# Luna attention and MoE on one core: v of batch 1 loaded ahead of its q, and another order of steps

## The chip, the cores and the metric

The kernel runs on one core of a Trainium2 chip. The time is that of the device for one execution, in microseconds (us). The engines are TensorE (PE; its weight loads are shown as PEld), VectorE (DVE), ScalarE (ACT), GpSimd (POOL) and SyncE (SP). Each works through its own instructions in their order in the program; semaphores make one wait for another.

## The reference

For 8 batches of 8 heads, with 576 positions of 64 channels and 32 packed positions:

```python
def sm_attn(qq, kk, vv):
    s = scale * np.matmul(qq, kk.transpose(0, 1, 3, 2))
    s = s - np.max(s, axis=-1, keepdims=True)
    a = np.exp(s)
    a = a / (np.sum(a, axis=-1, keepdims=True) + 1e-09)
    return np.matmul(a, vv)
p_packed = sm_attn(p, k, v)
out = sm_attn(q, p_packed, p_packed)
```

The result, with heads side by side as 4608 rows x of 512, goes through an MLP with 2048 hidden channels:

```python
h = x @ w_in
r = np.maximum(h, 0.0)
g = s * (r * r) + b
return (g @ w_out).astype(np.float32)
```

## The kernel before

The kernel works batch by batch. For a batch b it makes the scores of p against k and their exponentials, sums v with them into 32 packed values per head, scores q against the packed values, and normalizes. It does not form the attention's output: since that is weights times packed values, it multiplies the packed values by w_in first (`packed_w`, giving pw) and then pw by the weights (aT), which gives the hidden layer in one step (`mlp_in`). After relu and square (gT), 16 matmuls of 512 columns for each 128 rows give an output tile (`Out.step`, the yps rows of the profile).

The order is written out by hand. Each of PE's, DVE's, ACT's, POOL's and SP's instructions is pinned to the order in which the program issues it, and a string of words gives that order. In the profile nearly every instruction therefore bears a helper's line (L62 for matmuls, L65 for transposes, L73 for the rest). The words, with b the batch:

- `Lk`, `Lq`, `Lv`, `Lp1`, `Lpall`, `Lwi`, `Lwo`: loads on POOL's DMA queue (w_in and w_out in quarters; a quarter of w_out serves four of an output tile's 16 matmuls). Each of kn, qn and vn has one buffer, so that a load waits until the batch before has been read. Each load also waits for the landing of the one eight before it.
- `Tkb.h`, `Tqb.h`: transposes of half of k or q on PE and their copy to kT or qT; batches 0 and 1 only. `Dk`, `Dq`: the same by a transposing DMA on SP for the later batches.
- `PD`, `PP`, `PA`, `PPA`: doubling of p and its transposes, of batch 0 and 1 and of all others.
- `V`: copy of v into vr on DVE. `Fb.a`: first scores and their exponential. `P`: the packed values on PE (pps), their reciprocal and scaling on DVE (pk). `X`: two transposes of pk and the copy to ppd. `S`: second scores and their exponentials on ACT.
- `Ab.a`: sums of the exponentials on PE, then logarithm (ld) and reciprocal (rcd) on ACT and their product aT on DVE; in batch 0 by halves of the columns, with the product in a word of its own, `G0.h`.
- `Wb.c`: packed values times w_in into pw, one chunk of 512 columns in batch 0 and two in the others. Chunk 0 of batch 0 is copied in two halves; `E` is the second.
- `h0.m.h` and `Mb.m`: the hidden layer of two times 128 channels for half of the columns, or of 128 channels for all 576, each four matmuls of 288 columns, then relu on ACT (some on DVE) and square on DVE.
- `Ob.txn`: the next n of the 16 matmuls of output tile t. `BT`, `BC`: sums over w_out's rows for the bias, copied by DVE to biasrep, multiplied on PE and scaled by DVE.
- `Zn`: n matmuls of zeros, 512 columns, whose result nobody reads. `Yn`: the same into the PSUM buffer that the next step will take.

PSUM has two pools: psh with two buffers of two banks (the tiles hps, taken in turn by T, F, S, A, W, h, M, BT and BC, each freed by the engine that reads it), and psy with four (output tiles, packed values, single W chunks and Z).

Up to the string stand the loads of batch 0, the constants and 12 Z. After it the last output tile is done in two halves.

Of the kernel before, what the change touches and what calls it, by code (L numbers as in the profile page):

```python
# [14 lines left out]
def kernel(  # L15
# [14 lines left out]
    B, H, S, D = q.shape  # L30
# [3 lines left out]
    P = 128  # L34
# [10 lines left out]
    HS = S // 2  # L45
# [9 lines left out]
    ysp = ctx.enter_context(tc.tile_pool(name="ysp", bufs=3))  # L55
# [5 lines left out]
    def mm(*a, **kw):  # L61
        return tc.keep_in_program_order(nc.tensor.matmul(*a, **kw))  # L62
# [12 lines left out]
    vec, act, pool, sp = (Pinned(e) for e in (nc.vector, nc.scalar, nc.gpsimd, nc.sync))  # L75
# [280 lines left out]
    def packed_w(b, chs):  # L356
        if b not in pw:
            pw[b] = atp.tile([P, 2, DFF], BF16, tag="pw", name="pw")
        where = {}
        if len(chs) > 1:  # L360
            pair = [big() for _ in range(2)]
            where = {(a, x): pair[a][:, x, :] for a in range(2) for x in range(2)}
        if len(chs) != 2:
            single = [psy.tile([P, NB], F32, tag="y", name="wps") for _ in range(2)]
            where.update({(a, len(chs) - 1): single[a][:] for a in range(2)})
        for x, ch in enumerate(chs):
            for g in range(4):
                for a in range(2):
                    mm(
                        where[a, x][NP * g:NP * g + NP],  # L370
                        ppd[b % 2][D * a:D * a + D, a, g, :],
                        w_in_sb[D * a:D * a + D, g, ch * NB:(ch + 1) * NB],
                        start=True,
                        stop=True,
                        tile_position=(D * a, NP * g),
                    )
        if len(chs) > 1:
            for a in range(2):
                dst = pw[b][:, a, chs[0] * NB:(chs[0] + 2) * NB].rearrange("p (i f) -> p i f", f=NB)
                evict(dst, pair[a][:], a == 0)  # L380
        if len(chs) != 2:
            ch = chs[-1]
            if ch == 0:
                s2["w"] = single
                first_w(b, 0)
                return
            for a in range(2):
                evict(pw[b][:, a, ch * NB:(ch + 1) * NB], single[a][:], a == 0)

    def first_w(b, half):  # L390

        cols = slice(2 * P * half, 2 * P * half + 2 * P)
        for a in range(2):
            vec.tensor_copy(out=pw[b][:, a, cols], in_=s2["w"][a][:, cols])

    def evict(out, in_, on_act):
        if on_act:
            act.copy(out=out, in_=in_)
        else:
            vec.tensor_copy(out=out, in_=in_)  # L400


    def slot(b):
        return 1 if b % 2 else (b % 4)
# [4 lines left out]
    def mlp_in_half(b, m, hf):  # L409

        hps = big()
        cols = slice(hf * HS, (hf + 1) * HS)
        for i in range(2):
            for a in range(2):
                mm(
                    hps[:, i, 0:HS],
                    pw[b][:, a, (m + i) * P:(m + i + 1) * P],
                    aT[b][:, a, cols],
                    start=(a == 0),
                    stop=(a == 1),  # L420
                )
        rlu = ysp.tile([P, 2, HS], BF16, tag="rlu", name="rlu")
        if hf == 0 and m == 0:
            vec.tensor_scalar_max(out=rlu[:], in0=hps[:, :, 0:HS], scalar1=0.0)
        else:
            act.activation(out=rlu[:], in_=hps[:, :, 0:HS], func=AF.Relu)
        g0 = slot(b) * S + hf * HS
        vec.tensor_tensor(out=gT[:, m:m + 2, g0:g0 + HS], in0=rlu[:], in1=rlu[:], op=ALU.mult)

    def mlp_in(b, m):  # L430
        hps = big()
        for a in range(2):
            for hf in range(2):
# [7 lines left out]
        rlu = ysp.tile([P, 2, HS], BF16, tag="rlu", name="rlu")
        if b == 0 and m % 4 == 2:
            vec.tensor_scalar_max(out=rlu[:], in0=hps[:, :, 0:HS], scalar1=0.0)
        else:
            act.activation(out=rlu[:], in_=hps[:, :, 0:HS], func=AF.Relu)
        g0 = slot(b) * S
        vec.tensor_tensor(
            out=gT[:, m, g0:g0 + S].rearrange("p (a s) -> p a s", a=2),
            in0=rlu[:], in1=rlu[:], op=ALU.mult,
        )  # L450
# [118 lines left out]
    def run(word):  # L569
# [71 lines left out]
        out=identb[:], in_=identb[:], compare_op=ALU.not_equal, fill=1.0, base=0,  # L641
# [19 lines left out]
    idle(12, NB)  # L661

    for word in """
        Lwi0 Lwi1 Lwi2 Lwi3 Lwo0 Lwo1 Lp1 Tk0.0 Z10 PD Tk0.1 Lk1 PP0 Z3 F0.0 V0.0 F0.1 Z5 P0.0 V0.1 P0.1
        Z2 Tq0.0 Z1 X0 Z1 Tq0.1 Lq1 Lv1 Lwo2 Lwo3 Lpall Z4 S0 Z3 A0.0 W0.0 Z1 A0.1 G0.0 E Z1 h0.0.0 W0.1
        G0.1 h0.2.0 Y2 h0.0.1 h0.2.1 W0.2 M0.4 W0.3 M0.5 M0.6 O0.0x1 M0.7 O0.0x3 M0.8 M0.9 O0.1x1 PD1
        O0.0x1 M0.10 M0.11 O0.0x3 O0.1x1 PP1 M0.12 O0.1x2 Tk1.0 Tk1.1 Lk2 O0.1x2 M0.13 O0.1x1 F1.0
        O0.1x1 Tq1.0 O0.2x1 Tq1.1 O0.2x1 F1.1 O0.2x2 V1 Lv2 Lq2 M0.14 P1.1 M0.15 O0.2x3 O0.0x2 X1 O0.0x2
        O0.1x1 S1 O0.1x3 O0.2x1 BT PA A1.0 O0.0x3 BC A1.1 O0.1x3 O0.2x3 W1.0 O0.0x1 O0.1x1 O0.2x5 W1.2
        V2 O0.3x6 M1.0 PPA M1.1 M1.2 Dq2 Dk2 Lk3 Lv3 Lq3 O0.3x9 M1.3 M1.4 O0.3x1 O1.0x1 M1.5 M1.6 O1.0x2  # L670
        M1.7 M1.8 O1.0x2 M1.9 M1.10 O1.0x2 M1.11 M1.12 O1.0x2 M1.13 M1.14 O1.0x2 M1.15 O1.0x2 F2.0 F2.1
        O1.0x3 O1.1x3 P2.1 O1.1x5 X2 O1.1x3 S2 O1.1x4 A2.0 O1.1x1 O1.2x1 A2.1 O1.2x7 W2.0 O1.2x8 O1.3x1
        V3 O1.3x1 W2.2 O1.3x6 M2.0 O1.3x1 M2.1 O1.3x1 M2.2 O1.3x1 M2.3 Dq3 Dk3 Lk4 Lv4 Lq4 O1.3x1 M2.4
        O1.3x1 M2.5 O1.3x1 M2.6 O1.3x1 M2.7 O1.3x1 M2.8 O1.4x1 M2.9 O1.4x1 M2.10 O1.4x1 M2.11 O1.4x1
        M2.12 O1.4x1 M2.13 O1.4x1 M2.14 O1.4x1 M2.15 O1.4x9 O2.0x6 F3.0 F3.1 O2.0x6 P3.1 O2.0x4 O2.1x1
        X3 O2.1x5 W3.0 O2.1x6 W3.2 O2.1x4 O2.2x2 S3 O2.2x4 A3.0 O2.2x2 V4 A3.1 O2.2x8 O2.3x8 M3.0 M3.1
        Dq4 Dk4 Lk5 Lv5 Lq5 O2.3x2 M3.2 M3.3 O2.3x2 M3.4 M3.5 O2.3x2 M3.6 M3.7 O2.3x2 M3.8 M3.9 O3.0x2
        M3.10 M3.11 O3.0x2 M3.12 M3.13 O3.0x2 M3.14 M3.15 O3.0x8 F4.0 F4.1 O3.0x2 O3.1x4 P4.1 O3.1x5 X4
        O3.1x3 S4 O3.1x4 A4.0 O3.2x2 A4.1 O3.2x7 W4.0 O3.2x7 O3.3x2 V5 W4.2 O3.3x6 M4.0 O3.3x2 M4.1 M4.2
        O3.3x2 M4.3 Dq5 Dk5 Lk6 Lv6 Lq6 O3.3x4 M4.4 M4.5 O3.4x2 M4.6 M4.7 O3.4x2 M4.8 M4.9 O3.4x2 M4.10  # L680
        M4.11 O3.4x2 M4.12 M4.13 O3.4x2 M4.14 M4.15 O3.4x6 O4.0x6 F5.0 F5.1 O4.0x6 P5.1 O4.0x4 O4.1x1 X5
        O4.1x5 S5 O4.1x4 A5.0 O4.1x2 A5.1 O4.1x4 O4.2x3 W5.0 O4.2x7 V6 O4.2x5 W5.2 O4.2x1 O4.3x5 M5.0
        M5.1 O4.3x2 M5.2 Dq6 Dk6 Lk7 Lv7 Lq7 M5.3 O4.3x2 M5.4 M5.5 O4.3x2 M5.6 M5.7 O4.3x2 M5.8 M5.9
        O4.3x2 M5.10 M5.11 O4.3x1 O5.0x1 M5.12 M5.13 O5.0x2 M5.14 M5.15 O5.0x12 F6.0 F6.1 O5.0x1 O5.1x5
        P6.1 O5.1x5 X6 O5.1x3 S6 O5.1x3 O5.2x1 A6.0 O5.2x2 A6.1 O5.2x7 W6.0 O5.2x6 O5.3x3 V7 W6.2 O5.3x6
        M6.0 O5.3x2 M6.1 M6.2 O5.3x2 M6.3 Dq7 Dk7 M6.4 O5.3x2 M6.5 M6.6 O5.3x1 O5.4x1 M6.7 M6.8 O5.4x2
        M6.9 M6.10 O5.4x2 M6.11 M6.12 O5.4x11 M6.13 M6.14 O6.0x2 M6.15 O6.0x5 F7.0 F7.1 O6.0x6 P7.1
        O6.0x3 O6.1x2 X7 O6.1x4 S7 O6.1x4 A7.0 O6.1x2 A7.1 O6.1x4 O6.2x3 W7.0 O6.2x12 W7.2 O6.2x1 O6.3x5
        M7.0 M7.1 O6.3x2 M7.2 M7.3 O6.3x2 M7.4 M7.5 O6.3x2 M7.6 M7.7 O6.3x2 M7.8 M7.9 O6.3x2 M7.10 M7.11
        O6.3x1 O7.0x1 M7.12 M7.13 O7.0x2 M7.14 M7.15 O7.0x13 O7.1x16 O7.2x16 O7.3x16 O7.4x16  # L690
    """.split():
        run(word)
    while not todo[B - 1, NT].done:
# [29 lines left out]
```

## Time and profile before

| | |
|---|---|
| median of 6 runs | 250.93 us (250.44 to 251.0) |
| the profiled execution | 250.98 us |
| its span in the profile | 249.2 us |
| PE busy | 235.9 us (95%), 2251 matmuls recorded |
| DVE busy | 144.3 us (58%) |
| ACT busy | 138.9 us (56%) |
| POOL busy | 29.1 us (12%) |
| output matmuls (yps) | 138.4 us busy |
| hidden-layer matmuls (hps from aT, pw) | 76.3 us busy |
| zero matmuls (zps) recorded | 40, 12.9 us busy |
| chain that ended last | PE 80%, DMA 16% |

The span runs from the first to the last recorded instruction; about 1.8 us of the time lie around it. Matmuls are pipelined, so the busy time of one, 0.37 us for 512 columns, is longer than the distance from its start to the next start; where PE is the bound, the distance counts. A few matmul records are missing in the trace, which makes some distances look doubled. A row of the timeline gives start and duration in us, engine, line, operation, output and inputs with their shape, how many were merged, and in brackets the idle time of the engine before it with what ended it.

### The profile page before, as it was taken

What the parts mean: (1) busy time and instruction counts of PE and PEld (TensorE: products, weight loads), DVE (VectorE), ACT (ScalarE), POOL (GpSimd) and SP (SyncE); (2) the same over time, 40 slices, a digit from 0 to 9 for tenths busy, and PEclk for the clock granted to TensorE, in tenths of its full rate; (3) what the DMA queues carried; (4) which work ended last, traced back from release to release, by engine and by line L of the source; (5) the groups of instructions that cost most, each with busy time, mean ns of one, the idle gap of its engine ahead of it and who ended that gap; (6) DMA issues with size and microseconds to landing.
All of it is one profiled execution on the core that took longest, in us unless ns stands there. A gap on an engine that the chain in (4) does not pass through costs nothing.

```text
span 249.2 us, 5458 instructions
## 1 busy us (share of the span) xinstructions
PE 235.9 (95%) x2251; PEld 132.5 (53%) x2291; DVE 144.3 (58%) x278; ACT 138.9 (56%) x218; POOL 29.1 (12%) x43
## 2 busy tenths in 40 slices
PE   8796998999999999999999999999999999999994
PEld 2452565446653665356544665466545654366453
DVE  4338768399638673566548672577347642767221
ACT  2156753558856882568655763678375844577000
POOL 8642212000300030000300030000200000000000
PEclk9999999999999999999999999999999999999999
DMA  3999999999498969429898959468996911121133
GB/s 31 199 205 206 204 204 205 196 203 207 90 203 182 208 97 216 110 56 140 153 223 173 214 74 223 91 122 142 164 235 149 143 42 45 42 46 42 42 87 86
DMA packets 59450, 35.50 MB, mean 142 GB/s; under 512 B 32160, under 2 KB 54944, under 8 KB 59424
## 3 DMA queue, kind: packets, MB, share of 16 engines
q0 software_dynamic: 25184, 18.61, 50.1%
q1 hardware_dynamic: 34192, 16.49, 29.4%
q8 instruction: 18, 0.29, 0.5%
q14 instruction: 8, 0.07, 0.1%
q10 hardware_dynamic: 48, 0.03, 0.0%
HBM read 37.23 MB, written 9.44 MB: 187 GB/s over the span
## 4 chain that ended last, share of the span: by engine, by line
PE 80%; DMA 16%; issue 2%; POOL 0%; DVE 0%; POOLq 0%
PE yps L62 48%; PE hps L62 31%; DMA w_out_sb<-in_moe_w_out_dram 8%; DMA w_in_sb<-in_moe_w_in_dram 6%; DMA kn<-in_k_dram 3%; PE pps L62 1%; PE pps L65 1%; POOL kn L73 0%; DVE ysb L73 0%; POOL identb L73 0%; POOLq L73 0%; POOLq L707 0%
## 5 line engine op out<-in xcount | busy, mean ns | idle before, releaser
L62 PE MATMUL yps<-w_out_sb,gT 128*128 128x512 bf16 (+1 forms) x555 | 138.4, 373 | 3.7 <-issue 2.1
L73 ACT ACTIVATE rlu<-hps 128x576 bf16<-128x576 f32 x124 | 75.6, 649 | 28.5 <-PE hps L62 25.8
L62 PEld LDWEIGHTS <-gT 128*128 128x128 bf16 x592 | 54.8, 98 | 50.0 <-issue 8.0
L62 PE MATMUL hps<-aT,pw 128*128 128x288 bf16 x512 | 76.3, 285 | 2.5 <-DVE aT L73 2.3
L73 DVE TENSOR_TENSOR gT<-rlu 128x576 bf16<-128x576 bf16 x128 | 58.0, 458 | 31.0 <-ACT rlu L73 27.4
L62 PEld LDWEIGHTS <-pw 128*128 128x128 bf16 x512 | 49.4, 97 | 29.4 <-issue 4.4
L73 DVE SCALAR_TENSOR_TENSOR ysb<-yps,svec,biasrep 128x512 f32<-128x512 f32 (+1 forms) x37 | 26.9, 733 | 22.4 <-PE yps L62 18.1
L73 ACT ACTIVATE e<-hps 96x768 bf16<-96x768 f32 (+2 forms) x34 | 21.8, 693 | 30.3 <-PE hps L62 30.2
L73 ACT CAST pw<-hps 128x1024 bf16<-128x1024 f32 x14 | 14.2, 1012 | 16.4 <-PE hps L62 15.7
L73 DVE TENSOR_TENSOR aT<-e,rcd 128x576 bf16<-128x576 bf16 x16 | 12.1, 756 | 18.0 <-ACT rcd L73 18.0
L73 POOL DMA_DIRECT2D kn<-in_k_dram x9 | 6.9, 770 | 129.9 <-DMA kT<-kn 101.1
L73 DVE CAST pw<-hps 128x1024 bf16<-128x1024 f32 x14 | 17.1, 1219 | 2.7 <-PE hps L62 2.7
L62 PE MATMUL zps<-zb 128*128 128x512 bf16 x40 | 12.9, 450 | 1.6 <-DVE zb L73 1.2
L73 ACT ACTIVATE ld<-hps 128x576 f32<-128x576 f32 x16 | 10.3, 643 | 2.3 <-PE hps L62 1.6
L73 ACT ACTIVATE rcd<-ld 128x576 f32<-128x576 f32 x16 | 10.9, 683 | 0.5
L62 PEld LDWEIGHTS <-ppd 64*32 64x32 bf16 x384 | 3.5, 89 | 10.3 <-issue 6.9
L62 PE MATMUL hps<-w_in_sb,ppd 64*32 64x512 bf16 x224 | 8.8, 381 | 0.0
L73 DVE RECIPROCAL rd<-pps 128x2 f32<-128x2 f32 x8 | 1.4, 170 | 12.6 <-PE pps L62 12.6
L62 PEld LDWEIGHTS <-kT 128*128 128x128 bf16 x192 | 6.9, 98 | 2.4 <-issue 0.6
L73 DVE COPY vr<-vn 96x3072 bf16<-96x3072 bf16 (+1 forms) x9 | 7.7, 860 | 0.3 <-DMA vn<-in_v_dram 0.3
L62 PEld LDWEIGHTS <-zb 128*128 128x128 bf16 x45 | 4.5, 110 | 6.4 <-issue 3.2
L73 POOL DMA_DIRECT2D vn<-in_v_dram x9 | 6.8, 751 | 7.2 <-DVE vr L73 4.6
(58 smaller groups left out, 100.7 us busy)
## 6 DMA issues: line engine op xcount, KB each, us to landing
out_dram<-ysb SPq DMA_DIRECT2D x23, 192.0 KB, 2.5
kn<-in_k_dram POOLq DMA_DIRECT2D x7, 576.0 KB, 6.4
qn<-in_q_dram POOLq DMA_DIRECT2D x7, 576.0 KB, 12.5
vn<-in_v_dram POOLq DMA_DIRECT2D x7, 576.0 KB, 9.2
out_dram<-ysb SPq DMA_DIRECT2D x24, 128.0 KB, 2.4
w_in_sb<-in_moe_w_in_dram POOLq DMA_DIRECT2D x4, 512.0 KB, 13.6
w_out_sb<-in_moe_w_out_dram POOLq DMA_DIRECT2D x4, 512.0 KB, 18.8
out_dram<-ysb SPq DMA_DIRECT2D x23, 64.0 KB, 2.0
```

The source lines that it names most:

```text
L62: return tc.keep_in_program_order(nc.tensor.matmul(*a, **kw))
L65: return tc.keep_in_program_order(nc.tensor.transpose(*a, **kw))
L73: return lambda *a, **kw: tc.keep_in_program_order(f(*a, **kw))
```

## The change

Three things change in the code. `mlp_in_half` and `mlp_in` share a new function for relu and square; `packed_w` asks for batch 0 before it takes its branch for chunk 0; and the string of words is another one.

In the opening, `Lv1` moves from behind `Lq1` to behind `V0.1`, so that v of batch 1 is issued before its q. The fillers are spread differently: 33 Z in the string instead of 31, and 11 Y instead of 2. `W0.1` stands before `E` and `h0.0.0`, `W0.2` before `h0.0.1`, `W0.3` before `M0.4`. In batch 1 both `Tq` stand behind `P1.1`, and their second half first; `F1.1` follows `F1.0` with one output matmul between; `V1` and `M0.14`, `M0.15` stand before `P1.1`; `A1.0` stands before `BT`, `A1.1` before `BC`. In batch 2, `M1` steps and output matmuls alternate one by one, and `W2.0` is later. The later batches have other places too, with the same steps: in batch 3, S and A before W; in batches 4 and 6, W before or around S; in batch 7, `W7.2` behind `M7.7`, and the first three output tiles interleaved with the last hidden steps.

The code, cut:

```diff
-            if ch == 0:
+            if b == 0 and ch == 0:
                 s2["w"] = single
                 first_w(b, 0)
                 return
...
+    def squared(out, hps, on_vec):
+
+        h = hps[:, :, 0:HS]
         rlu = ysp.tile([P, 2, HS], BF16, tag="rlu", name="rlu")
-        if hf == 0 and m == 0:
-            vec.tensor_scalar_max(out=rlu[:], in0=hps[:, :, 0:HS], scalar1=0.0)
+        if on_vec:
+            vec.tensor_scalar_max(out=rlu[:], in0=h, scalar1=0.0)
         else:
-            act.activation(out=rlu[:], in_=hps[:, :, 0:HS], func=AF.Relu)
-        g0 = slot(b) * S + hf * HS
-        vec.tensor_tensor(out=gT[:, m:m + 2, g0:g0 + HS], in0=rlu[:], in1=rlu[:], op=ALU.mult)
+            act.activation(out=rlu[:], in_=h, func=AF.Relu)
+        vec.tensor_tensor(out=out, in0=rlu[:], in1=rlu[:], op=ALU.mult)
```

The string, up to batch 2 and at the places of the later batches that are spoken of:

```diff
-        Lwi0 Lwi1 Lwi2 Lwi3 Lwo0 Lwo1 Lp1 Tk0.0 Z10 PD Tk0.1 Lk1 PP0 Z3 F0.0 V0.0 F0.1 Z5 P0.0 V0.1 P0.1
-        Z2 Tq0.0 Z1 X0 Z1 Tq0.1 Lq1 Lv1 Lwo2 Lwo3 Lpall Z4 S0 Z3 A0.0 W0.0 Z1 A0.1 G0.0 E Z1 h0.0.0 W0.1
-        G0.1 h0.2.0 Y2 h0.0.1 h0.2.1 W0.2 M0.4 W0.3 M0.5 M0.6 O0.0x1 M0.7 O0.0x3 M0.8 M0.9 O0.1x1 PD1
-        O0.0x1 M0.10 M0.11 O0.0x3 O0.1x1 PP1 M0.12 O0.1x2 Tk1.0 Tk1.1 Lk2 O0.1x2 M0.13 O0.1x1 F1.0
-        O0.1x1 Tq1.0 O0.2x1 Tq1.1 O0.2x1 F1.1 O0.2x2 V1 Lv2 Lq2 M0.14 P1.1 M0.15 O0.2x3 O0.0x2 X1 O0.0x2
-        O0.1x1 S1 O0.1x3 O0.2x1 BT PA A1.0 O0.0x3 BC A1.1 O0.1x3 O0.2x3 W1.0 O0.0x1 O0.1x1 O0.2x5 W1.2
-        V2 O0.3x6 M1.0 PPA M1.1 M1.2 Dq2 Dk2 Lk3 Lv3 Lq3 O0.3x9 M1.3 M1.4 O0.3x1 O1.0x1 M1.5 M1.6 O1.0x2
...
+        Lwi0 Lwi1 Lwi2 Lwi3 Lwo0 Lwo1 Lp1 Tk0.0 Z10 PD Tk0.1 Lk1 PP0 Z3 F0.0 V0.0 F0.1 Z5 P0.0 V0.1 Lv1
+        P0.1 Z1 Tq0.0 Z1 X0 Z2 Tq0.1 Lq1 Lwo2 Lwo3 Lpall Z3 S0 Z3 A0.0 Z2 W0.0 Z2 A0.1 G0.0 Z1 W0.1 E Y1
+        h0.0.0 G0.1 Y4 h0.2.0 W0.2 Y4 h0.0.1 Y1 h0.2.1 W0.3 Y1 M0.4 M0.5 M0.6 O0.0x1 M0.7 O0.0x3 M0.8
+        M0.9 O0.1x1 PD1 O0.0x1 M0.10 M0.11 O0.0x3 O0.1x1 PP1 M0.12 O0.1x2 Tk1.1 Tk1.0 Lk2 O0.1x2 M0.13
+        O0.1x1 F1.0 V1 Lv2 O0.1x1 F1.1 O0.2x2 M0.14 O0.2x1 M0.15 P1.1 O0.2x1 Tq1.1 Tq1.0 Lq2 O0.2x1 X1
+        O0.2x3 O0.0x3 S1 O0.0x1 O0.1x3 A1.0 O0.1x1 BT PA A1.1 O0.0x3 O0.1x3 BC O0.2x4 W1.0 O0.0x1 O0.1x1
+        O0.2x4 W1.2 V2 O0.3x6 M1.0 PPA M1.1 M1.2 Dq2 Dk2 Lk3 Lv3 Lq3 O0.3x9 M1.3 O0.3x1 M1.4 O1.0x1 M1.5
...
+        O5.1x5 X6 O5.1x4 W6.0 O5.1x1 O5.2x5 W6.2 O5.2x6 S6 O5.2x4 A6.0 O5.2x1 O5.3x1 A6.1 V7 O5.3x15
+        M6.0 M6.1 O5.4x1 Dq7 Dk7 O5.4x1 M6.2 M6.3 O5.4x2 M6.4 M6.5 O5.4x2 M6.6 M6.7 O5.4x2 M6.8 M6.9
...
+        O6.0x2 O6.1x3 X7 O6.1x4 S7 O6.1x4 A7.0 O6.1x2 A7.1 O6.1x3 O6.2x16 W7.0 O6.3x7 M7.0 M7.1 O6.3x2
+        M7.2 M7.3 O6.3x2 M7.4 M7.5 O6.3x2 M7.6 M7.7 O6.3x3 O7.0x8 W7.2 O7.1x7 M7.8 M7.9 O7.1x1 O7.2x1
+        M7.10 M7.11 O7.0x2 M7.12 M7.13 O7.0x2 M7.14 M7.15 O7.0x2 O7.1x2 O7.0x1 O7.1x2 O7.0x1 O7.1x4
+        O7.2x15 O7.3x16 O7.4x16
```

More of the change, by code (lines that the diff above doesn't have):

```diff
@@ L421, in mlp_in_half @@
                 )
+        g0 = slot(b) * S + hf * HS
+        squared(gT[:, m:m + 2, g0:g0 + HS], hps, hf == 0 and m == 0)
+    def squared(out, hps, on_vec):
+        h = hps[:, :, 0:HS]
         rlu = ysp.tile([P, 2, HS], BF16, tag="rlu", name="rlu")
-        if hf == 0 and m == 0:
-            vec.tensor_scalar_max(out=rlu[:], in0=hps[:, :, 0:HS], scalar1=0.0)
-        else:
-            act.activation(out=rlu[:], in_=hps[:, :, 0:HS], func=AF.Relu)
-        g0 = slot(b) * S + hf * HS
-        vec.tensor_tensor(out=gT[:, m:m + 2, g0:g0 + HS], in0=rlu[:], in1=rlu[:], op=ALU.mult)
+        if on_vec:
+            vec.tensor_scalar_max(out=rlu[:], in0=h, scalar1=0.0)
+        else:
+            act.activation(out=rlu[:], in_=h, func=AF.Relu)
+        vec.tensor_tensor(out=out, in0=rlu[:], in1=rlu[:], op=ALU.mult)
     def mlp_in(b, m):
@@ L440, in mlp_in @@
                 )
[L441 to L445, printed above, removed]
         g0 = slot(b) * S
[L447 to L450, printed above, removed]
+        squared(gT[:, m, g0:g0 + S].rearrange("p (a s) -> p a s", a=2), hps, b == 0 and m % 4 == 2)
     bias = {}
@@ L669 @@
-        O0.1x1 S1 O0.1x3 O0.2x1 BT PA A1.0 O0.0x3 BC A1.1 O0.1x3 O0.2x3 W1.0 O0.0x1 O0.1x1 O0.2x5 W1.2
-        V2 O0.3x6 M1.0 PPA M1.1 M1.2 Dq2 Dk2 Lk3 Lv3 Lq3 O0.3x9 M1.3 M1.4 O0.3x1 O1.0x1 M1.5 M1.6 O1.0x2
-        M1.7 M1.8 O1.0x2 M1.9 M1.10 O1.0x2 M1.11 M1.12 O1.0x2 M1.13 M1.14 O1.0x2 M1.15 O1.0x2 F2.0 F2.1
-        O1.0x3 O1.1x3 P2.1 O1.1x5 X2 O1.1x3 S2 O1.1x4 A2.0 O1.1x1 O1.2x1 A2.1 O1.2x7 W2.0 O1.2x8 O1.3x1
-        V3 O1.3x1 W2.2 O1.3x6 M2.0 O1.3x1 M2.1 O1.3x1 M2.2 O1.3x1 M2.3 Dq3 Dk3 Lk4 Lv4 Lq4 O1.3x1 M2.4
@@ L674 @@
[L674 to L682, printed above, removed]
-        M5.1 O4.3x2 M5.2 Dq6 Dk6 Lk7 Lv7 Lq7 M5.3 O4.3x2 M5.4 M5.5 O4.3x2 M5.6 M5.7 O4.3x2 M5.8 M5.9
@@ L684 @@
[L684 to L688, printed above, removed]
@@ L689 @@
-        M7.0 M7.1 O6.3x2 M7.2 M7.3 O6.3x2 M7.4 M7.5 O6.3x2 M7.6 M7.7 O6.3x2 M7.8 M7.9 O6.3x2 M7.10 M7.11
-        O6.3x1 O7.0x1 M7.12 M7.13 O7.0x2 M7.14 M7.15 O7.0x13 O7.1x16 O7.2x16 O7.3x16 O7.4x16
+        Lwi0 Lwi1 Lwi2 Lwi3 Lwo0 Lwo1 Lp1 Tk0.0 Z10 PD Tk0.1 Lk1 PP0 Z3 F0.0 V0.0 F0.1 Z5 P0.0 V0.1 Lv1
+        P0.1 Z1 Tq0.0 Z1 X0 Z2 Tq0.1 Lq1 Lwo2 Lwo3 Lpall Z3 S0 Z3 A0.0 Z2 W0.0 Z2 A0.1 G0.0 Z1 W0.1 E Y1
+        h0.0.0 G0.1 Y4 h0.2.0 W0.2 Y4 h0.0.1 Y1 h0.2.1 W0.3 Y1 M0.4 M0.5 M0.6 O0.0x1 M0.7 O0.0x3 M0.8
@@ new lines @@
+        M0.9 O0.1x1 PD1 O0.0x1 M0.10 M0.11 O0.0x3 O0.1x1 PP1 M0.12 O0.1x2 Tk1.1 Tk1.0 Lk2 O0.1x2 M0.13
+        O0.1x1 F1.0 V1 Lv2 O0.1x1 F1.1 O0.2x2 M0.14 O0.2x1 M0.15 P1.1 O0.2x1 Tq1.1 Tq1.0 Lq2 O0.2x1 X1
+        O0.2x3 O0.0x3 S1 O0.0x1 O0.1x3 A1.0 O0.1x1 BT PA A1.1 O0.0x3 O0.1x3 BC O0.2x4 W1.0 O0.0x1 O0.1x1
+        O0.2x4 W1.2 V2 O0.3x6 M1.0 PPA M1.1 M1.2 Dq2 Dk2 Lk3 Lv3 Lq3 O0.3x9 M1.3 O0.3x1 M1.4 O1.0x1 M1.5
+        O1.0x1 M1.6 O1.0x1 M1.7 O1.0x1 M1.8 O1.0x1 M1.9 O1.0x1 M1.10 O1.0x1 M1.11 O1.0x1 M1.12 O1.0x1
@@ new lines @@
+        M1.13 O1.0x1 M1.14 O1.0x1 M1.15 O1.0x3 F2.0 F2.1 O1.0x2 O1.1x4 P2.1 O1.1x5 X2 O1.1x4 S2 O1.1x3
+        O1.2x1 A2.0 O1.2x2 A2.1 O1.2x13 W2.0 O1.3x2 V3 O1.3x5 W2.2 O1.3x6 M2.0 M2.1 O1.3x2 M2.2 Dq3 Dk3
+        Lk4 Lv4 Lq4 M2.3 O1.3x1 O1.4x1 M2.4 M2.5 O1.4x2 M2.6 M2.7 O1.4x2 M2.8 M2.9 O1.4x2 M2.10 M2.11
+        O1.4x2 M2.12 M2.13 O1.4x7 M2.14 M2.15 O2.0x7 F3.0 F3.1 O2.0x6 P3.1 O2.0x3 O2.1x2 X3 O2.1x4 S3
+        O2.1x4 A3.0 O2.1x2 A3.1 O2.1x4 O2.2x3 W3.0 O2.2x8 V4 O2.2x4 W3.2 O2.2x1 O2.3x5 M3.0 M3.1 O2.3x2
@@ new lines @@
+        M3.2 Dq4 Dk4 Lk5 Lv5 Lq5 M3.3 O2.3x2 M3.4 M3.5 O2.3x2 M3.6 M3.7 O2.3x2 M3.8 M3.9 O2.3x2 M3.10
+        M3.11 O2.3x1 O3.0x1 M3.12 M3.13 O3.0x2 M3.14 M3.15 O3.0x12 F4.0 F4.1 O3.0x1 O3.1x16 P4.1 O3.2x6
+        X4 O3.2x4 W4.0 O3.2x6 S4 O3.3x4 A4.0 V5 O3.3x2 A4.1 O3.3x7 W4.2 O3.3x3 O3.4x3 M4.0 Dq5 Dk5 Lk6
+        Lv6 Lq6 O3.4x3 M4.1 M4.2 O3.4x2 M4.3 M4.4 O3.4x2 M4.5 M4.6 O3.4x2 M4.7 M4.8 O3.4x2 M4.9 M4.10
+        O3.4x2 M4.11 M4.12 O4.0x2 M4.13 M4.14 O4.0x2 M4.15 O4.0x3 F5.0 F5.1 O4.0x6 P5.1 O4.0x3 O4.1x2 X5
@@ new lines @@
+        O4.1x4 S5 O4.1x4 A5.0 O4.1x2 A5.1 O4.1x4 O4.2x3 W5.0 O4.2x8 V6 O4.2x4 W5.2 O4.2x1 O4.3x5 M5.0
+        M5.1 O4.3x2 M5.2 Dq6 Dk6 Lk7 Lv7 Lq7 M5.3 O4.3x2 M5.4 M5.5 O4.3x2 M5.6 M5.7 O4.3x2 M5.8 M5.9
+        O4.3x2 M5.10 M5.11 O4.3x1 O5.0x1 M5.12 M5.13 O5.0x2 M5.14 M5.15 O5.0x13 F6.0 F6.1 O5.1x6 P6.1
+        O5.1x5 X6 O5.1x4 W6.0 O5.1x1 O5.2x5 W6.2 O5.2x6 S6 O5.2x4 A6.0 O5.2x1 O5.3x1 A6.1 V7 O5.3x15
+        M6.0 M6.1 O5.4x1 Dq7 Dk7 O5.4x1 M6.2 M6.3 O5.4x2 M6.4 M6.5 O5.4x2 M6.6 M6.7 O5.4x2 M6.8 M6.9
@@ L691 @@
+        O5.4x2 M6.10 M6.11 O5.4x2 M6.12 M6.13 O5.4x2 M6.14 M6.15 O5.4x2 O6.0x8 F7.0 F7.1 O6.0x6 P7.1
+        O6.0x2 O6.1x3 X7 O6.1x4 S7 O6.1x4 A7.0 O6.1x2 A7.1 O6.1x3 O6.2x16 W7.0 O6.3x7 M7.0 M7.1 O6.3x2
+        M7.2 M7.3 O6.3x2 M7.4 M7.5 O6.3x2 M7.6 M7.7 O6.3x3 O7.0x8 W7.2 O7.1x7 M7.8 M7.9 O7.1x1 O7.2x1
+        M7.10 M7.11 O7.0x2 M7.12 M7.13 O7.0x2 M7.14 M7.15 O7.0x2 O7.1x2 O7.0x1 O7.1x2 O7.0x1 O7.1x4
+        O7.2x15 O7.3x16 O7.4x16
     """.split():
```

## The prediction

> **What bounds the kernel now.** I read the engine shares first, then busy time by stage, then TensorE's (PE's) rows in order of time, and last the DMA issues, because a stage that waits for data has to be told from one that waits for an engine. The stages are cut where the work changes: the first output matmul (28.5), the landing of the third quarter of w_out (43.2) and the end of batch 1's preparation (55.5). Columns: stretch and length, then busy time and instructions of each engine, granted clock, DMA share, GB/s.
>
> ```profile
> 0.00:28.50 28.50, 22.92 (x246) 11.79 (x250) 15.07 (x40) 12.95 (x23) 14.34 (x24) 1.00 1.06 167
> 28.50:43.20 14.70, 13.54 (x177) 9.08 (x181) 11.31 (x24) 6.80 (x12) 3.30 (x4) 1.00 1.30 203
> 43.20:55.50 12.30, 12.06 (x121) 5.32 (x123) 7.98 (x13) 6.37 (x9) 0.00 (x0) 1.00 1.34 198
> 55.50:249.20 193.70, 187.35 (x1711) 106.29 (x1739) 109.93 (x204) 112.82 (x176) 11.50 (x15) 1.00 0.69 131
> ```
>
> From 55.5 on PE is the bound: the gap from one output matmul's start to the next is 0.216, and in this stretch almost every gap is exactly that of its kind. So the 193.7 us there cannot shrink by reordering. Before 55.5 a second bound is visible: the DMA engines move some 200 GB/s without a pause. What can be won lies in PE's idle rows before that (start, duration, engine, line, operation; in brackets idle time before it and what ended it):
>
> ```profile
> 21.39 0.65 PE L62 MATMUL hps<-aT,pw 128*128 128x288 bf16 x4 [1.13 <-DVE aT L73]
> ...
> 24.64 1.14 PE L62 MATMUL hps<-aT,pw 128*128 128x288 bf16 x8 [1.17 <-DVE aT L73]
> ...
> 28.51 0.38 PE L62 MATMUL yps<-w_out_sb,gT 128*128 128x512 bf16 x1 [0.25 <-DMA w_out_sb<-in_moe_w_out_dram]
> ...
> 41.12 0.55 PE L62 MATMUL pps<-vr,e 96*32 96x65 bf16 x48 [0.59 <-DVE vr L73]
> ...
> 43.23 0.59 PE L62 MATMUL yps<-w_out_sb,gT 128*128 128x512 bf16 x2 [0.31 <-DMA w_out_sb<-in_moe_w_out_dram]
> ```
>
> The third and fifth are gates: PE stands until a piece of w_out has landed, so time saved ahead of a gate is lost in it. That is the heart of this forecast.
>
> **The refactoring costs nothing.** `squared` issues the same two instructions as before. The added `b == 0` changes no instruction, as every later batch calls `packed_w` with two chunks and never enters that branch.
>
> **The DMA queue.** The loads all leave through POOL's queue, in order. Before, q of batch 1 is issued at 18.12 and v at 21.40:
>
> ```profile
> 18.12 0.78 POOL L73 DMA_DIRECT2D qn<-in_q_dram  x1 [1.69 <-PE hps L62]
> 21.40 0.77 POOL L73 DMA_DIRECT2D vn<-in_v_dram  x1 [2.50 <-DVE aT L73]
> 23.72 0.77 POOL L73 DMA_DIRECT2D w_out_sb<-in_moe_w_out_dram  x1 [1.55 <-DMA w_in_sb<-in_moe_w_in_dram]
> ```
>
> By the trace's times to landing (19.0, 18.7 and 19.5 us, the longest of each tensor in this stretch) they land at 37.1, 40.1 and 43.2. Here row and rule differ. The Trainium skill, "DMA: Bandwidth & Descriptors", section "Anatomy of one DMA", gives about 2.0 us plus bytes over 436 kB per us. For 576 KB that is 3.4 us: q and v would be there by 25 us, 16 us before use, and the swap would be worth exactly nothing. The rule is for a transfer alone; here each stands behind megabytes. I take the row. After the swap v lands at 37.1 and q at 40.1. The w_out pieces follow the same bytes, so they stay at 43.2 and 45.1. Batch 2's v is issued behind V1 (about 39.0, was 41.36) and its q behind Tq1.0 (about 41.6, was 42.12). Neither lands sooner, since the queue is full of earlier bytes; neither holds up SP, whose first transposing DMA is at 56.4.
>
> **Up to the first output matmul.** Fillers go from 43 Z and 2 Y to 45 and 11: 11 more by 0.216 = 2.4 us if nothing hid them. They stand in the two aT stalls and the 0.25 at the gate, 2.55 us of idle. Followed row by row: one Z less ahead of S0 starts it at 17.25 (was 17.46); A0.0, behind its exponentials, at 18.52 (18.73). Two Z put W0.0 at 19.29 (19.06) and, with one more, A0.1 at 20.07 (19.63). On VectorE (DVE) the first pw casts start 0.45 after W0.0, at 19.77 (19.54). aT's first half follows at 20.57 as before, because ScalarE (ACT) has its reciprocal earlier and the casts later. The moved W0.1 waits for w_in's second quarter, due near 20.84, runs at 20.95, and its cast (0.60 to the next start) goes ahead of E (0.80), relu (0.80) and gT (0.38). aT's second half starts at 24.01 (23.85), and h0.0.1 behind it at 24.80 (24.64). Then W0.3, four M-sized groups, and ACT's queue of two relus, a cast and a relu (0.6 each) give M0.6 at 28.05 and the first output matmul at 28.55, against 28.51. **Cost: 0.04**, since the fillers lie inside the stalls. Without that cover they cost up to 2.4.
>
> Do the fillers buy clock? The first row above shows the granted clock at 1.00 through stalls of 1.1 us. The skill, "TensorE: Matmul & The Clock Gate", section Part 1, says an idle window of about 3.4 us halves it. By that rule alone one cold window in these stalls would cost 1.7 us and the fillers would save it; by the row nothing was lost, so nothing is saved.
>
> **28.5 to the gate at 43.2.** Up to there PE does what it did, plus one output matmul (24 instead of 23) and the two transposes of X1: 0.22 + 0.11 = 0.33 more. The stall of 0.59 for vr goes: v lands at 37.1, V1 runs 38.0 to 39.0 behind gT of M0.13, P1.1 starts near 39.9. What is late next: F1.1 now follows F1.0 with one matmul between and takes the buffer of M0.13, whose relu ends at 37.53: 0.1. Tq1.1 reaches PE at 40.65, q landed at 40.1. X1 waits for pk, about 0.1. PE is at the gate at 42.75, as before, and stands until 43.22. So it arrives with 0.33 more done and **0.47 of slack**, which also absorbs the 0.04.
>
> **43.2 to 52.6.** S1 starts at 44.18 (was 44.51): 43.22 and three output matmuls, with 0.31 for the last as before every S. Its last start, 44.33, plus 0.22 and four output matmuls gives A1.0 at 45.43, and one more BT at 45.98, after w_out's last quarter (45.1). A1.0 now goes before BT, so aT's first half (0.66 to the next start) stands in front of the biasrep copy on DVE. Before, the copy was first:
>
> ```profile
> 46.95 0.69 DVE L73 COPY biasrep<-hps 128x512 f32<-128x512 f32 x1 [2.69 <-PE hps L62]
> 47.55 0.41 DVE L73 COPY pall<-pall 96x1024 bf16<-96x1024 bf16 x1
> 48.68 0.76 DVE L73 TENSOR_TENSOR aT<-e,rcd 128x576 bf16<-128x576 bf16 x1 [0.71 <-ACT rcd L73]
> 49.35 0.75 DVE L73 TENSOR_SCALAR biasrep<-hps,bvec 128x512 f32<-128x512 f32 x1
> ```
>
> After: ACT does two exponentials (44.57 to 45.76), then ld and reciprocal of A1.0 to 47.23; aT 47.27; copy 47.93 to 48.6; BC cannot start before 48.7, though PE is there at 48.5. BC and four output matmuls end at 50.5. W1.0 needs BC's buffer, which DVE frees only after pall, aT and the scaling (49.86 to 50.6): W1.0 at 50.66. Before it stood at 50.29 with one output matmul less, so at 50.51 for equal work: **0.15 late.** W1.2 stands at 52.6 with the same matmuls behind it as at 52.46 before. The 0.33 has been spent in these handovers.
>
> **From there on.** Both versions have the same matmuls left after p's transposes. Three more pairs of M stand next to each other, at 0.153 instead of 0.122: 0.09. For new stalls I compared the work between dependent steps with the shortest distance that ran without one. X to S grows in batches 2, 4 and 6 from 0.65 us to 0.86 and more. Two places are shorter than any before: A6.1 to M6.0 (3.24 against 3.46), and W7.0 to M7.0 with seven output matmuls. There DVE needs 0.45 + 1.22 = 1.67 and PE gives 0.31 + 1.51 = 1.82. I cost both at nothing; ends 0 to 0.7 each.
>
> **Sum** against the profiled execution, 250.98 us around a span of 249.2: +0.15 +0.09 = +0.24, so **251.2 us**. The median of the runs before is 250.93, 0.05 lower. About 0.2%, 0.5 us, is what a measurement of this kernel can tell from no change.
>
> **Rivals.**
> - *Gain (chance 0.12).* The 0.33 survives: DVE and ACT hand over 0.3 sooner than my latencies, and the 0.21 that BC waited goes too. That gives -0.55, 250.4 us. More is not to be had while w_out lands at 43.2. For it: the vr stall is on PE and does go. Against: the DVE order at biasrep.
> - *Slower by fillers (0.20).* One filler block holds PE when aT is ready. It decides once h0.0.1 starts after 25.3, when the 0.47 of slack is used. With half of the 2.55 us cover lost: 2.4 - 1.3 - 0.47 = 0.6, with the sum 251.8. For it: eight fillers stand in two blocks of four, and DVE's order holds aT back. Against: aT at 24.8 comes after the last filler's end by my rows, if barely.
> - *Slower later (0.12).* The thin places of batches 6 and 7 stall by up to 0.7 each, near 252.2 to 252.6.
> - *The forecast (0.56):* between -0.25 and +0.5, 250.7 to 251.5.
>
> From these come faster 0.12, same 0.56, slower 0.32. The range 250.4 to 252.2 leaves out the far ends of the first and third rival.
>
> **What would show it.** The first output matmul near 28.5; no idle time before P1.1; a w_out wait of about 0.5 near 43.2; W1.2 near 52.6; from 55.5 a remainder of 193.7 to 193.9. It is wrong if w_out's third piece lands at another time, if the first output matmul is later than 29.0, or if a releaser other than "issue" appears on PE after 56.

## The result, and the profile after

The changed kernel takes 250.6 us in the median (250.39 to 253.07, 35 runs) against 251.0 us before (250.36 to 251.96, 72 runs); the ratio is 0.9994, with a 95% interval of 0.9986 to 1.0002. That is 0.15 us less, with 0.35 less to 0.05 more in the interval: no change that the measurement can tell. The forecast was 0.24 more. The ratio weighs all runs, and the times of either kernel stand in groups: 12 of the 35 runs of the changed kernel and 21 of the 72 of before lie above 251.3 us, a group whose cause (lost clock) is traced below. Without it the medians are 250.56 and 250.96 us, 0.40 less for the changed kernel. A lower group of before, ten runs at 250.36 to 250.53, is in no trace.

The profiled execution of the changed kernel took 250.53 us around a span of 248.8. Its stages, in the columns of the first fence of the prediction:

```profile
0.00:28.50 28.50, 24.93 (x256) 12.95 (x261) 15.15 (x40) 13.25 (x23) 14.34 (x24) 1.00 1.06 166
28.50:43.20 14.70, 14.00 (x185) 9.37 (x186) 11.42 (x24) 6.60 (x11) 3.31 (x4) 1.00 1.30 204
43.20:55.50 12.30, 11.88 (x121) 5.26 (x121) 7.89 (x12) 6.67 (x10) 0.00 (x0) 1.00 1.36 203
55.50:249.00 193.50, 187.14 (x1707) 105.92 (x1735) 109.71 (x204) 112.20 (x175) 11.50 (x15) 1.00 0.68 131
```

PE is busier by 2.0 us before 28.5, and the time has not changed: busy time there is filler in place of idle time. The last stretch is cut at round numbers. From the start of the last of p's transposes to the start of the last output matmul it is 190.02 us before (55.45 to 245.47) and 189.93 after (55.13 to 245.06). So 0.32 us comes from the opening and 0.09 from all later batches. The row of p's transposes, before and then after, is earlier by the same 0.32:

```profile
54.81 0.84 PE L65 MATMUL pps<-identb,pall 96*128 96x96 bf16 x16
54.49 0.84 PE L65 MATMUL pps<-identb,pall 96*128 96x96 bf16 x16
```

PE's rows in the changed kernel around the two gates, and those that the forecast names:

```profile
28.81 0.38 PE L62 MATMUL yps<-w_out_sb,gT 128*128 128x512 bf16 x1 [0.16 <-DMA w_out_sb<-in_moe_w_out_dram]
...
39.84 0.56 PE L62 MATMUL pps<-vr,e 96*32 96x65 bf16 x48
40.56 1.19 PE L65 MATMUL hps<-identb,qn 96*128 96x96 bf16 x24 [0.16 <-DVE gT L73]
...
41.98 1.71 PE L62 MATMUL yps<-w_out_sb,gT 128*128 128x512 bf16 x6
43.62 0.44 PE L62 MATMUL hps<-qT,ppd 64*32 64x288 bf16 x16
...
48.21 1.10 PE L62 MATMUL hps<-biasrep,rowsf 128*128 128x512 f32 x2
49.14 1.03 PE L62 MATMUL yps<-w_out_sb,gT 128*128 128x512 bf16 x4
50.10 0.67 PE L62 MATMUL hps<-w_in_sb,ppd 64*32 64x512 bf16 x16
```

P1.1 (39.84) has no idle time ahead of it any more; the 0.59 for vr is gone. The wait for w_out's third quarter hides inside the merged row at 41.98: six output matmuls and the 0.31 ahead of S would take 5 x 0.216 + 0.31 = 1.39, and S1 comes 1.64 later. The 0.25 is the wait; the quarter landed at 42.84 and the matmul started at 42.88.

### The profile page after: what moved, and what is told of

Same layout as the page of the kernel before. It is cut to its first block, busy times and chain, and to the rows that moved or that the text cites. A ratio compares the mean times of both kernels' runs of the same rounds, so it can differ in the third digit from the quotient of the medians.

```text
span 248.8 us, 5482 instructions
## 1 busy us (share of the span) xinstructions
PE 237.9 (96%) x2262; PEld 133.5 (54%) x2302; DVE 144.2 (58%) x278; ACT 138.7 (56%) x218; POOL 29.2 (12%) x43
## 4 chain that ended last, share of the span: by engine, by line
PE 80%; DMA 16%; issue 2%; ACT 1%; POOL 0%; DVE 0%; POOLq 0%
PE yps L62 47%; PE hps L62 31%; DMA w_out_sb<-in_moe_w_out_dram 8%; DMA w_in_sb<-in_moe_w_in_dram 6%; DMA kn<-in_k_dram 3%; PE pps L62 1%; PE pps L65 1%; POOL kn L73 0%; ACT rcd L73 0%; ACT ld L73 0%; DVE ysb L73 0%; POOL identb L73 0%; POOLq L73 0%; POOLq L705 0%
## 5 line engine op out<-in xcount | busy, mean ns | idle before, releaser
L62 PE MATMUL zps<-zb 128*128 128x512 bf16 x42 | 13.5, 444 | 1.3 <-DVE zb L73 1.2
L62 PEld LDWEIGHTS <-zb 128*128 128x128 bf16 x56 | 5.4, 107 | 7.4 <-issue 3.9
L62 PE MATMUL hps<-pbd,kT 128*128 128x64 bf16 x192 | 7.1, 193 | 0.4 <-ACT pbd L73 0.2
```

## The experiments

Each kernel differs from the one named by the edit shown. All traces and times are of one core, as before. The expectations use short names: e1 is the swap alone, e5 the order of before up to W1.2 with the new rest, e7 the bias copy ahead of aT, e9 that kernel with 16 Z, e11 the kernel before with 16 Z. Where a granted clock is given for a whole run, 0.993 is what one window of 3.41 us at half clock makes of some 249 us.

### The swap alone

In the kernel before, only the two loads change places:

```diff
-        Z2 Tq0.0 Z1 X0 Z1 Tq0.1 Lq1 Lv1 Lwo2
+        Z2 Tq0.0 Z1 X0 Z1 Tq0.1 Lv1 Lq1 Lwo2
```

> The kernel before with one edit: v of batch 1 is issued ahead of q, all else in its old place. Theory (each load stands behind the bytes ahead of it, so the one issued second lands near 40.1 us): Tq1.0, which PE reached at 37.6, now waits until 40.2; the vr stall of 0.59 goes, and the slack of about 0.5 before the wait for w_out's third quarter is used up: first matmul that needs that quarter near 44.7 instead of 43.2, so about 252.4 us. Rival 1 (a load lands some 3.4 us after its issue, the queue does not matter): no change, 250.9. Rival 2 (the wait for w_out hides all that is late before it): 250.9, with that matmul still at 43.2.

It took 253.88 us (252.64 to 254.06, 4 runs), ratio 1.0100 (1.007 to 1.013). Three rows of its trace, PE's wait for q and then two windows of 3.41 us:

```profile
40.06 0.69 PE L65 MATMUL hps<-identb,qn 96*128 96x96 bf16 x12 [2.47 <-DMA qn<-in_q_dram]
```

```profile
37.84:41.25 3.41, 1.19 (x24) 1.07 (x25) 0.62 (x2) 0.38 (x1) 0.00 (x0) 1.00 1.26 206
41.25:44.66 3.41, 3.19 (x48) 1.95 (x49) 2.08 (x4) 0.81 (x1) 1.13 (x2) 0.50 1.54 194
```

Both rivals fall: the load issued second landed at 40.02, 2.4 us after PE wanted it. But the loss, 2.9 us, is twice the 1.5 of the theory. The third column from the end is the granted clock: after a window in which PE was busy for only 1.19 us, the next ran at half.

The same kernel with the wait filled tells the two parts of the loss apart:

```diff
         split = b == 0 and what == "q"
+        if b == 1 and what == "q" and half == 0:
+            for _ in range(10):
+                mm(tp[0].bitcast(F32), zb[:, 0:P], zb[:, 0:NB], start=True, stop=True)
```

> As e1_swap_only, with ten matmuls of zeros (2.1 us) in the place where PE waits for q of batch 1. Theory (e1 lost 2.9 us, of which the wait beyond the slack is 1.5 and the half clock in the window from 41.2 to 44.7 the rest): the granted clock stays 1.00 and the time is near 252.3, 1.5 less than e1 with ten matmuls more. Rival (the clock is not what it costs): 253.9 as e1.

252.61 us (252.59 to 253.69, 4 runs), ratio 1.0067 (1.0043 to 1.009). The clock stayed at 1.00 in the trace and in three of the four runs; the fourth, with 0.993, is the 253.69. The wait itself stayed (q's transposes start at 40.1), and 1.27 us went with the half clock. The swap alone says the same: three of its runs have 0.993 of the clock, and the one with all of it took 252.64.

### The new order with q first again

```diff
-        V0.1 Lv1 P0.1
+        V0.1 P0.1
...
-        Tq0.1 Lq1 Lwo2
+        Tq0.1 Lq1 Lv1 Lwo2
```

> The changed kernel with q of batch 1 issued ahead of v again. Theory: v lands near 40.1; V1 at 40.2 holds DVE, P1.1 starts near 41.2 (39.8 in the changed kernel), pk near 43.9, S1 near 45.7 (43.6), so 2.0 us later than the changed kernel: 252.6 us. Rival (the wait for w_out's third quarter at 42.9 hides it): as the changed kernel, 250.6.

251.82 us (251.77 to 251.88, 10 runs), ratio 1.0032 (1.0023 to 1.0041): 1.2 us more than the changed kernel, where 2.0 were expected.

```profile
41.06 0.55 PE L62 MATMUL pps<-vr,e 96*32 96x65 bf16 x48 [1.34 <-DVE vr L73]
```

P1.1 stands where it was expected (41.2), but X1 is at 43.31 instead of 43.9 and S1 at 44.84 instead of 45.7: DVE took less time behind V1 than I had given it. So the swap and the new places of V, Tq and P belong together: against the kernel before, the swap in the old order costs 2.9 us (1.3 of it the clock), the new order without the swap 0.8, and both together nothing that the ratio can tell. Two of the ten runs have 0.992 and 0.993 of the clock and took no longer, 251.85 and 251.82. If that clock went ahead of the wait for vr, the wait hid it; no trace shows where it went.

### Without the Y fillers

All 11 `Y` words are taken out of the changed string.

> The changed kernel without its 11 Y. Theory: they lie in stalls for aT and in front of w_out's first quarter; the first output matmul stays near 28.8, the wait for the third quarter ends near 42.9, granted clock 1.00: 250.6 us, within 0.3. Rival 1 (the fillers are on the path): 2.4 us less, 248.2, the first output matmul near 28.8 but the rest earlier. Rival 2 (they keep the clock): the granted clock falls to half for a window of some 3.4 us, 1.7 us more, 252.3.

250.68 us (250.59 to 251.14, 20 runs), ratio 0.9989 (0.9982 to 0.9995), which overlaps the interval of the changed kernel. In its trace the clock stayed at 1.00, and the first output matmul waits for the same landing:

```profile
29.12 0.38 PE L62 MATMUL yps<-w_out_sb,gT 128*128 128x512 bf16 x1 [0.82 <-DMA w_out_sb<-in_moe_w_out_dram]
```

So at full clock the Y were neither on the path nor needed for the clock: in the emptiest window of this stretch (20.64 to 24.05), PE was still busy for 2.35 us of 3.41. In the six runs with 0.993 of the clock the median is 251.12, and 251.38 in the eleven such runs of the changed kernel. So the Y may cost up to 0.26 us there; no trace shows it.

### Without the load of q of batch 1

Batch 1 takes batch 0's q, which is still in the buffer; its own is not loaded.

```diff
+        elif word == "Lq1":
+            raw["q", 1] = raw["q", 0]
         elif what in ("Lk", "Lq", "Lv"):
```

> The changed kernel without the load of q of batch 1: its q is that of batch 0, still in the buffer. 590 KB less stand ahead of w_out's third quarter, which should land about 2.9 us earlier, near 40.0. Theory (PE reaches the place at 42.6 anyway): the wait of 0.25 goes and no more, 250.3 us. Rival (the DMA stream bounds the opening): up to 2.9 us less, 247.8.

250.2 us (250.08 to 251.41, 20 runs), ratio 0.9976 (0.9964 to 0.9987). w_out's third quarter landed at 39.6, 3.2 us earlier, and the gain over the changed kernel is 0.4: the wait and little more.

```profile
41.81 1.46 PE L62 MATMUL yps<-w_out_sb,gT 128*128 128x512 bf16 x6
43.23 0.44 PE L62 MATMUL hps<-qT,ppd 64*32 64x288 bf16 x16
```

The six matmuls and the switch now take 1.42 us, against 1.64 with the wait. In the changed kernel the DMA stream (the row of loads that fills the opening) is therefore a gate that PE reaches a quarter of a microsecond early, not a bound with microseconds behind it.

### The opening and the rest apart

Both orders have done the same work at W1.2, so the string can be cut there: the new opening with the old rest, and the reverse.

The first of the two against the changed kernel, with the first line that differs; from `W1.2` to the end the words are those of the string before:

```diff
-        O0.2x4 W1.2 V2 O0.3x6 M1.0 PPA M1.1 M1.2 Dq2 Dk2 Lk3 Lv3 Lq3 O0.3x9 M1.3 O0.3x1 M1.4 O1.0x1 M1.5
+        O0.2x4 W1.2 V2 O0.3x6 M1.0 PPA M1.1 M1.2 Dq2 Dk2 Lk3 Lv3 Lq3 O0.3x9 M1.3 M1.4 O0.3x1 O1.0x1 M1.5
...
```

In the second it is the other way round.

> The changed order up to W1.2, then the order of before, at a place where both have done the same work. Theory: the opening brings 0.3 us in the trace (p's transposes end at 55.1 instead of 55.45) and the rest 0.1, so this kernel is 0.3 faster than before, ratio near 0.9988. Rival (the later order makes the difference): as before, ratio 1.000.

> The order of before up to W1.2, then the changed one. Theory: 0.1 us faster than before at most, ratio 0.9996 to 1.0004, p's transposes at 55.45. By my prediction's count of neighbouring M pairs it would be 0.09 slower. Rival (the later order makes the difference): 0.3 to 0.4 faster, ratio 0.9985.

Over all runs these are inconclusive: 250.71 us (14 runs) and 250.97 us (13 runs), both 0.9995 (0.9984 to 1.0006). The granted clock of each run sorts them. In the runs without a lost window the medians are 250.69 us (10 runs) for the new opening and 250.86 (8 runs) for the new rest, against 250.98 (30 runs) for the kernel before: 0.29 and 0.12 less, near the 0.3 and 0.1 of the two theories. The traces agree. The new opening ends p's transposes at 55.13 here as well. From there to the last output matmul the old rest took 190.08, and in five other traces with that order 190.02 to 190.04; the new rest took 189.93 here and 189.93 to 189.96 in seven others. So the later order is worth 0.1 us, and not the 0.09 loss that I had counted.

### Batch 1's bias copy ahead of aT

In the changed kernel, the sequence of before for BT, A1.0, BC and A1.1:

```diff
-        O0.1x3 A1.0 O0.1x1 BT PA A1.1 O0.0x3 O0.1x3 BC O0.2x4 W1.0
+        O0.1x4 BT PA A1.0 O0.0x3 BC A1.1 O0.1x3 O0.2x4 W1.0
```

> The changed kernel with BT, A1.0, BC and A1.1 in the sequence of before, so that the biasrep copy is ahead of aT on DVE. Theory (the lead of 0.3 that batch 1 brings is spent because aT holds back the copy and so BC): BC waits 0.2 us less, W1.0 near 49.9 instead of 50.1, 0.2 faster than the changed kernel, ratio to before near 0.9985. Rival (the handovers cost the same in either order): as the changed kernel.

250.33 us (250.2 to 251.13, 22 runs), ratio 0.9979 (0.997 to 0.9988): faster than before, and than the changed kernel (250.29 against 250.56 in the runs that kept the clock). First DVE's rows in the changed kernel, then PE's in this one:

```profile
46.70 0.76 DVE L73 TENSOR_TENSOR aT<-e,rcd 128x576 bf16<-128x576 bf16 x1 [3.36 <-ACT rcd L73]
47.38 0.68 DVE L73 COPY biasrep<-hps 128x512 f32<-128x512 f32 x1
47.98 0.41 DVE L73 COPY pall<-pall 96x1024 bf16<-96x1024 bf16 x1
48.31 0.75 DVE L73 TENSOR_TENSOR aT<-e,rcd 128x576 bf16<-128x576 bf16 x1
49.34 0.75 DVE L73 TENSOR_SCALAR biasrep<-hps,bvec 128x512 f32<-128x512 f32 x1 [0.28 <-PE hps L62]
```

```profile
47.13 1.09 PE L62 MATMUL hps<-biasrep,rowsf 128*128 128x512 f32 x2
...
49.91 0.62 PE L62 MATMUL hps<-w_in_sb,ppd 64*32 64x512 bf16 x16
```

In the changed kernel DVE waited 3.36 us for ACT's reciprocal and only then copied biasrep, so BC (48.21) came late and with it the scaling that frees BC's buffer. With the copy first, W1.0 stands 6.95 us behind the gate (42.96 here) instead of 7.22. That is the 0.27 of the handover.

### The kernel before once more, and four more Z

> The kernel before once more, for its trace. Two traces with the same loads in the opening had w_out's third quarter landed at 42.5, where the first trace of before had 43.19. Theory A (the landing differs from execution to execution): near 42.5 to 42.9 here, so that the wait at it is below 0.2 or gone and the lead that the first two traces show between the kernels (0.3 at p's transposes) is partly the landing's. Theory B (the order of the program sets it): 43.2 again.

This run took 251.56 us, and w_out's third quarter landed at 42.48, as in theory A. It also belongs to the upper group of times. Two windows of it:

```profile
4.34:7.75 3.41, 1.40 (x12) 0.55 (x10) 0.15 (x1) 0.00 (x0) 2.90 (x6) 1.00 1.06 145
7.75:11.16 3.41, 3.41 (x18) 1.53 (x15) 0.92 (x2) 0.00 (x0) 2.50 (x4) 0.50 1.38 199
```

PE has run out of Z before k lands and is busy for 1.40 us of 3.41; the next window runs at half clock, and the first output matmul is at 29.73 instead of 28.51. PE's first two rows in the first trace of before, and then in this one:

```profile
1.19 5.11 PE L62 MATMUL zps<-zb 128*128 128x512 bf16 x12 [1.19 <-DVE zb L73]
7.53 0.68 PE L65 MATMUL hps<-identb,kn 96*128 96x96 bf16 x12 [1.23 <-DMA kn<-in_k_dram]
```

```profile
1.19 4.30 PE L62 MATMUL zps<-zb 128*128 128x512 bf16 x12 [1.19 <-DVE zb L73]
7.50 0.95 PE L65 MATMUL hps<-identb,kn 96*128 96x96 bf16 x12 [2.01 <-DMA kn<-in_k_dram]
```

The same twelve Z end 0.8 us sooner in this one, and k lands no sooner. The first output matmul is 1.22 us late, but the upper group of before is only 0.6 us above the rest: the waits for vr and for w_out's third quarter hide half of the loss. Without the load of q of batch 1, where both waits are gone, the upper group (251.4) lies 1.2 us above the rest (250.2), the whole of it, if its clock is lost at the same place; no trace of that group was kept.

To cover the hole, the number of Z ahead of the string is raised in three kernels: the bias copy ahead of aT, the kernel before and the changed kernel, with one expectation each in this order.

```diff
-    idle(12, NB)
+    idle(16, NB)
```

> As e7_bt_first, with 16 Z instead of 12 ahead of the first transposes. The times of e7 stand in two groups, near 250.3 and 251.05, and one trace of an upper group (e5) has the granted clock at half from 7.4 to 10.8 us, after a window in which PE was busy for 1.32 of 3.41 us. Theory: the upper group comes from that window; four more Z fill it to some 2.0 us, and nearly all runs fall near 250.3. Rival (another cause): two groups as before, or all runs later by up to 0.9 (the four Z on the path).

> The kernel before with 16 Z instead of 12 ahead of the first transposes, nothing else. Theory (a half-clock window near 7.4 to 10.8 us costs the runs that fall into it about 0.6): the group of before near 251.5 goes, the groups near 250.5 and 251.0 stay, which differ by the landing of w_out's third quarter; ratio near 0.9990. Rival (it was the other order that made e9 fast): groups and ratio as before, 1.000.

> The changed kernel with 16 Z instead of 12, nothing else. Theory: its group near 251.4 goes and nearly all runs stand near 250.5, ratio to before near 0.9975; against e11 the change is then worth 0.1 to 0.4 us by itself. Rival: two groups as in the changed kernel, ratio 0.9994.

| with 16 Z | us, median (range, runs) | ratio to before (interval) |
|---|---|---|
| kernel before | 250.88 (250.57 to 250.95, 21) | 0.9988 (0.9982 to 0.9995) |
| changed kernel | 250.49 (250.31 to 250.61, 8) | 0.9977 (0.9966 to 0.9988) |
| bias copy ahead of aT | 250.16 (250.09 to 250.3, 5) | 0.9955 (0.9943 to 0.9968) |

No run of the three stands in an upper group: against the 1.4 us of before's runs in the same series, the range is 0.4 and less. In the last kernel the window from 5.8 us, in which k lands, is filled to 3.01 of 3.41 us. The medians of that table also give the change by itself, without the clock in the way: 0.39 us less. It agrees with the 0.40 of the runs above that kept the clock. Of the 21 runs of before with 16 Z, 20 are slower than every one of the changed kernel's 8.

## Why the prediction held, point by point

The range held, and so did the account of what bounds the kernel; the sum did not. It had +0.24. The measured ratio makes it -0.15, and the runs without lost clock -0.40, outside the forecast's own band of -0.25 to +0.5. That the measurement calls it no change was luck in part: over all runs the lost clock, which no part of the forecast had, blurs the gain.

**What bounds the kernel: right.** From 55.5 on the order moved 0.1 us in 190. Ahead of it, time saved before a landing was lost in it; the kernel without q's load shows that little more lies behind that gate.

**The refactoring: right.** Both profiles count 278 instructions on DVE and 218 on ACT, and the old rest in the new code took 190.08 us, against 190.02 to 190.04 in the old, 0.06 more at most.

**The DMA queue: right for q and v, off by 0.35 for w_out.** Position decides: the second of the two loads lands at 40.0 to 40.2 whichever it is. After the swap that is q, issued at 21.46 and landed at 40.20, 18.7 us later. So the row was to be preferred to the fit of the Trainium skill ("DMA: Bandwidth & Descriptors", section "Anatomy of one DMA"), whose 3.4 us for 576 KB leaves out what stands ahead in the queue. But w_out's third quarter landed at 42.84 and not at 43.2, which the prediction had named as a sign of being wrong; the sum below shows what that was worth.

**The fillers: right in what they cost.** S0 at 17.21 (forecast 17.25), W0.0 at 19.25 (19.29), h0.0.1 at 24.75 (24.80), M0.6 at 28.00 (28.05). The first output matmul was 0.26 later than forecast (28.81), because its quarter of w_out landed at 28.77 in this trace and not at 28.47. The slack at the gate behind it absorbed that. The slack was smaller than the forecast 0.47: PE waited 0.25 there.

**28.5 to the gate: right.** P1.1 39.84 (39.9), Tq1.1 40.56 (40.65).

**From the gate to W1.0: wrong in sign, by two terms.** The step was "W1.0 at 50.66 ... **0.15 late**". It stood at 50.10, 0.41 early against the 50.51 of equal work. Two terms make up the 0.56 between them. First, "so they stay at 43.2": the third quarter landed at 42.84 and PE went on at 42.88, 0.34 earlier than my 43.22. Second, a slip in "43.22 and three output matmuls, with 0.31": the 0.31 is counted from the last matmul's start, so only two of 0.216 belong in front of it; 0.22. Both fall ahead of S1, which came at 43.62 and not at 44.18, 0.56 early; W1.0 is early by the same 0.56. So the steps from S1 to W1.0 took what they were forecast to take. The mechanism was right: aT in front of the biasrep copy eats part of the lead, and moving the copy forward gave 0.27 back. W1.2 followed at 52.10, not 52.6.

**The rest of the kernel: sign wrong, by 0.18.** I had +0.09 from neighbouring M pairs; the traces give -0.09. Neither thin place stalled: M7.0 and M6.0 have no idle time ahead of them. Which small rows make up the 0.18 I have not settled.

**The rivals.** Slower by fillers and slower later did not happen. The gain rival was on the right side, but smaller than its 0.55 (0.15 in the measured ratio, 0.39 in the medians without the clock in the way), and not for its reason: the handovers between DVE and ACT were no cheaper than forecast, as the equal 0.56 at S1 and W1.0 shows. The lead came from the earlier landing, which the rival held fixed, and from the slip in the sum.

**The clock: right for the fillers of the change, and missed elsewhere.** That the Y bought no clock is shown. That the kernel loses clock in some executions at 7.5 us I had not seen, since the one trace of before was free of it.

One thing stays open. The third quarter of w_out lands at 43.1 to 43.2 in two traces of the order before (one with 16 Z), and at 42.5 in two others with the same loads in the same order, both of which had lost the clock at 7.4 to 7.8 us. It lands at 42.5 to 42.9 in all traces of the new opening with its loads, and at 42.5 to 42.6 in the two of the old order with the loads swapped. What decides it was not tried. So part of the 0.3 us by which the new opening leads, or all of it, may come through this landing and not through the places of the steps. The lower group of before, at 250.4 to 250.5, may be such a landing at full clock; no trace of it exists.

## What to carry to other kernels

Find the landings that PE waits for before pricing anything ahead of them: a saving there is worth at most the slack at the next landing, and what an early arrival brings can be spent again at the next handover between two engines, as with the bias copy behind aT. A load in a full queue is priced by the bytes ahead of it (576 KB less brought w_out's third quarter 3.2 us forward), so swapping two loads moves both, and their users must move along. And where a kernel's times fall in groups, sort the runs by their granted clock and look for a short, sparsely filled stretch of PE before trying another order: here the groups hid a gain of 0.4 us.

## What the runs showed of the hardware

The clock falls at a much smaller hole than I had assumed. Windows of 3.41 us with PE busy for 1.19, 1.32 and 1.40 us, 35 to 41%, were each followed by one of the same length at half clock. The idle gaps of PE that they held or cut into were 2.47, 2.12 and 2.01 us. Windows with 2.09 us (61%) and more kept it, among them those with the two aT stalls of the kernel before, and so did the emptiest such window of all traces (the very end, where PE runs out of work, apart), with 1.79 us (52%) and a gap of 1.62 us, in the kernel with the bias copy ahead of aT (it and the window behind it):

```profile
5.06:8.47 3.41, 1.79 (x19) 0.94 (x18) 0.28 (x1) 0.00 (x0) 2.93 (x5) 1.00 1.21 172
8.47:11.88 3.41, 3.23 (x30) 1.76 (x29) 1.69 (x4) 0.73 (x2) 2.22 (x3) 1.00 1.34 201
```

Between 41 and 52% nothing was measured, and these windows don't tell busy share from length of gap. I had weighed the rule of an idle window of about 3.4 us (the Trainium skill, "TensorE: Matmul & The Clock Gate", Part 1): the length agrees, but the window need not be idle throughout.

Where the windows start differs between executions, and with it how long the first Z take. They follow each other at 0.43 us until the first recorded window begins and at 0.22 from there. It begins at 5.99 us in the first trace of before and at 4.34 and 4.00 in the two traces that lost the clock near 7.5. So the twelve Z end at 6.3 us in the one and at 5.3 to 5.5 in the two, with k's transposes at 7.4 to 7.5 in each. The hole of 1.23 us cost nothing; those of 2.0 and 2.1 cost 0.5 to 0.8 in the runs' groups.
